# Fused attention and gated convolution on one core: attention products of a head pair moved into the next pair's slot, and all engines in written order

## The chip, the core and the metric

The program runs on one core of a Trainium2 chip. The core has a matrix engine (TensorE, PE in the profile; its weight loads are PEld), a vector engine (VectorE, DVE), an activation engine (ScalarE, ACT), a general engine (GpSimd, POOL) and SyncE (SP), which here only issues transfers. Each engine works through a list of instructions of its own and waits on semaphores for the others. The metric is the device time of one execution in microseconds (us); lower is better.

## What is computed

Eight batches, twelve heads, 448 positions, head width 64. An attention whose softmax has exp(-m) added to its denominator is followed by a projection into three parts, a circular convolution of the middle part along the sequence (written with FFTs), a product of the three parts, and an output projection:

```
scores = (1/sqrt(64)) * q @ k^T;  m = max(scores);  e = exp(scores - m)
attn   = e / (sum(e) + exp(-m) + 1e-09);   x = concat_heads(attn @ v)      # 8 x 448 x 768
x1, x2, x3 = split(x @ w_proj, 3)                                          # 768 -> 3*768
x2_conv = irfft(rfft(x2, axis=1) * rfft(filter_fft, axis=0), axis=1)
out = (x1 * x2_conv * x3) @ w_out
```

Multiplied through by exp(m), the denominator is 1 + sum(exp(scores)), so no maximum is taken. The FFTs are products with small sine and cosine tables.

## The kernel before

**Attention** goes by head pair `hp` (six to a batch). `transposes` (T in what follows) turns the pair's keys and queries by matmul into one PSUM tile and copies them with VectorE into a zero-padded key tile `kz` (two copies) and `qT`. `scores` is called four times: part 0 (S0) makes one matmul and one exp on ScalarE (`er`), parts 1 to 3 (S) two matmuls and one exp each (`e`); `er` and `e` are the numerators, transposed. `attn_out` (AV) is called for two halves of the queries: 14 matmuls into the tile `op`, of which there is one, then on VectorE `rec` (add 1, reciprocal) and the product `xb`. `back` (X, the way back) transposes `xb` and copies it into `xT`; GpSimd copies two columns of `xT`, and after every third pair VectorE folds `xT` into `xf` (`u`, `w`, four `xf` products: the folds).

**Dense work** of a batch is a list of units: 12 gate units (G: six matmuls of 448 columns; part 0 copied by ScalarE to `x1`, part 1 multiplied by VectorE into `g`), 8 projections (P: six matmuls of 384 columns, copied by ScalarE to `x2`), 4 spectrum units (Z: two matmuls, two ScalarE copies `xs`, four VectorE products into `yh`), 6 inverse units (V: four matmuls, ScalarE copy `cw`, and for each two of them three VectorE steps into `yT`) and 8 output units (W: six matmuls, ScalarE copy `osb`, a store for each two).

**PSUM**: two tiles for scores, one for `op`, three (tag `hy`) which T, X and all dense units share in turn.

**Order.** The main loop at the end walks through the attention units and after each takes dense units of the batch before from `queue`, in proportion to costs written by hand (RATIO 1.9). In a slot of a pair stand S0, T of the next pair, S, X of the pair before, S, S, AV, AV. `manual_schedule` keeps this order for TensorE and GpSimd; a scheduler orders VectorE, ScalarE and SyncE by its own estimate. Dense work of batch b starts in the first slot of batch b+1, once `filter_spectrum` (16 matmuls on a filter that is loaded by DMA, and its sums `uw` on VectorE) is done. After the last attention slot the dense work of batch 7 runs alone.

**Start.** `first_load` brings batch 0 as float32 through SyncE in per-pair tiles (three buffers to a kind); `first_casts` turns them into bf16 (keys VectorE, queries ScalarE, values GpSimd). `tables` makes the sine tables with VectorE and ScalarE. The later batches (`attn_load`), the weights and the filter come by casting DMAs from GpSimd's queue. Batch 0 has no dense work beside it.

Of the kernel before, what the change touches and what calls it, by code (L numbers as in the profile page):

```python
# [19 lines left out]
SP = 112  # L20
# [19 lines left out]
def kernel(  # L40
# [33 lines left out]
    make_identity(nc, ident_bf)  # L74
# [15 lines left out]
    for i in range(2):  # L90
        nc.vector.memset(kn[i][:, :, 0, :], 0.0)
        nc.vector.memset(vr[i], 0.0)
        nc.vector.memset(vn[i][:, :, :, DH : DH + 1], 1.0)
        for u in range(2):
            nc.vector.memset(vr[i][64 * u : 64 * u + 64, :, u, DH : DH + 1], 1.0)
    for i in range(3):
        nc.vector.memset(kz[i], 0.0)
# [34 lines left out]
    def first_load(sp, tp):  # L132


        A = batch_tiles(0)
        rows = {}
        for name, x in (("k", k), ("v", v)):
            y = rows[name] = x[0].rearrange("h s d -> (h s) d").rearrange("(g r) d -> r g d", r=896)
            R = A[f"s{name}r"] = tp.tile([128, NHP, DH], F32, name=f"s{name}r")
            nc.sync.dma_start(R, y[384:512])  # L140
        for hp in range(NHP):
            for name in ("k", "v"):
                t = A[f"s{name}", hp] = sp.tile([128, 2, 3, DH], F32, name=f"s{name}")
                for u in range(2):
                    nc.sync.dma_start(
                        t[:, u].rearrange("p j d -> p (j d)"),
                        rows[name][512 * u : 512 * u + 384, hp, :].rearrange(
                            "(p j) d -> p (j d)", j=3
                        ),
                    )  # L150
                if name == "k":
                    t = A["sq", hp] = sp.tile([SP, 2, NST, DH], F32, name="sq")
                    nc.sync.dma_start(
                        t[:].rearrange("p u j d -> p u (j d)"),
                        q[0, 2 * hp : 2 * hp + 2].rearrange("u (p j) d -> p u (j d)", j=NST),
                    )
        return A

    def first_rests(A):
        for u in range(2):  # L160
            c = slice(64 * u, 64 * u + 64)
            nc.vector.tensor_copy(A["kn"][c, :, 0, c], A["skr"][c])
            nc.gpsimd.tensor_copy(A["vr"][c, :, u, 0:DH], A["svr"][c])

    def first_casts(A, hp):
        nc.vector.tensor_copy(
            A["kn"][:, hp, 1:4, :].rearrange("p j (u d) -> p u j d", u=2), A["sk", hp]
        )
        nc.scalar.copy(
            A["qf"][:, :, 2 * hp : 2 * hp + 2, :].rearrange("p j u d -> p u j d"), A["sq", hp]  # L170
        )
        for u in range(2):
            nc.gpsimd.tensor_copy(
                A["vn"][:, hp, 4 * u : 4 * u + 3, 0:DH], A["sv", hp][:, u]
            )
# [99 lines left out]
    def filter_load():  # L275
        F = hyp.tile([FQ, 4, D], BF16, name="filt", tag="yh")
# [8 lines left out]
    def filter_spectrum(F):  # L285

        uw = hyp.tile([FQ, 2, 2, D], BF16, name="uw", tag="g")
# [26 lines left out]
    def transposes(A, hp):  # L314
# [18 lines left out]
        if A["b"] == 0:  # L333
# [48 lines left out]
    def back(A, hp):  # L382
# [9 lines left out]
        nc.gpsimd.tensor_copy(xT[:, hp, S : S + 2], xT[:, hp, 0:2])  # L392
        if hp % 3 == 2:
            ds = slice(hp - 2, hp + 1)
            u = fold.tile([128, 3, HALF + 2], BF16, name="u")
            w = fold.tile([128, 3, HALF + 2], BF16, name="w")
            lo, hi = xT[:, ds, 0 : HALF + 2], xT[:, ds, HALF : S + 2]
            nc.vector.tensor_tensor(u, lo, hi, op=ALU.add)
            nc.vector.tensor_tensor(w, lo, hi, op=ALU.subtract)
            for pg, (t, op) in enumerate(  # L400
                ((u, ALU.add), (u, ALU.subtract), (w, ALU.subtract), (w, ALU.add))
            ):
                nc.vector.tensor_tensor(
                    A["xf"][:, pg, ds, 0:FQ],
# [229 lines left out]
```

## Time and profile before

| | |
|---|---|
| median of three runs | 532.7 us (531.22 to 533.28) |
| profiled execution | 532.04 us, of which 530.3 us are the span of the profile |
| PE / PEld busy | 439.5 us (83%) / 299.5 us |
| DVE / ACT / POOL busy | 303.4 us (57%) / 292.7 us (55%) / 117.6 us (22%) |
| exp of a score pair `e` (L348), of `er` (L352) | 920 ns x144, 550 ns x48 |
| `rec` add (L373), reciprocal (L374), `xb` (L375) | 160, 176, 424 ns x96 each |
| folds `u` (L398), `w` (L399), `xf` (L403) | 509, 505 ns x16; 334 ns x64 |
| `xs` copy (L460), `x1` copy (L484), `g` product (L486) | 485, 537, 618 ns |
| first scores, batch 0: pair 0, pair 2, pair 3 | start at 21.28, 46.06, 53.20 us |
| matmuls of `filter_spectrum` | 76.02 to 79.53 us |
| memsets of one `kn`, `vr`, `vn` on VectorE | 0.38, 0.71, 0.09 and two in 0.19 us |

The mean durations are those of a group of like instructions. Neighbours on an engine overlap a little at their ends, so that starts lie closer together than the durations say. An idle time is put down to the engine or transfer whose semaphore came last. The granted clock of TensorE is a share of 2.4 GHz: 0.78 between 20 and 40 us, 0.71 between 40 and 60, 0.91 between 60 and 80, and 1.00 from there to 500 us.

### The profile page before, as it was taken

Reading aid. Unit: us, or ns where it says so; the run is one execution under the profiler, and the core shown is the slowest. Engines: PE = TensorE matmul, PEld = TensorE weight load, DVE = VectorE, ACT = ScalarE, POOL = GpSimd, SP = SyncE. Lnnn points to the kernel's source line nnn. Section 1 sums busy time; section 2 is a strip of 40 time slices with the busy share of each in tenths; the row PEclk is TensorE's granted clock in tenths of the full one; section 3 lists DMA queues with packets and bytes.
Section 4 is the critical chain, followed back from the end, with each engine's and each line's share of the span. In section 5 each row is a group of like instructions: output and inputs, shape, how many; then the busy total and the mean of one; then the engine's idle time right before and its main releaser. Section 6 shows DMA issues by size and latency. Waiting matters only on the chain.

```text
span 530.3 us, 9720 instructions
## 1 busy us (share of the span) xinstructions
PE 439.5 (83%) x3872; PEld 299.5 (56%) x3872; DVE 303.4 (57%) x881; ACT 292.7 (55%) x499; POOL 117.6 (22%) x184
## 2 busy tenths in 40 slices
PE   0254678989997899989997999989997999899995
PEld 0133456556664676556664667557664667466654
DVE  8624653685529744675538644674548654774170
ACT  2532465656565574665565565755665656745443
POOL 4447026000530018010620027000710000000000
PEclk9966899999999999999999999999999999999999
DMA  7999919300990039601990049401990030002003
GB/s 214 207 208 127 123 10 133 17 2 28 131 103 2 2 105 123 36 0 54 126 84 1 2 112 131 19 1 54 142 70 1 6 99 1 2 1 79 26 1 104
DMA packets 128685, 35.63 MB, mean 67 GB/s; under 512 B 117117, under 2 KB 125056, under 8 KB 128640
## 3 DMA queue, kind: packets, MB, share of 16 engines
q0 software_dynamic: 118080, 19.87, 50.1%
q1 hardware_dynamic: 10560, 15.14, 9.6%
q8 instruction: 30, 0.49, 0.4%
q14 instruction: 15, 0.12, 0.1%
HBM read 43.86 MB, written 11.01 MB: 103 GB/s over the span
## 4 chain that ended last, share of the span: by engine, by line
PE 52%; DVE 21%; ACT 13%; DMA 6%; issue 5%; SPq 1%; POOL 1%; ACTq 0%; DVEq 0%; POOLq 0%
PE ops L523 11%; PE pps L440 11%; PE pps L475 10%; ACT e L348 8%; PE op L365 6%; PE sc L346 5%; ACT cw L506 3%; DVE t L463 3%; DVE t L464 3%; DMA filt<-in_moe_filter_fft_dram 2%; PE op L360 2%; DVE xb L375 2%; PE xps L388 2%; DMA sv<-in_v_dram 2%; DVE g L486 2%
## 5 line engine op out<-in xcount | busy, mean ns | idle before, releaser
L348 ACT ACTIVATE e<-sc 128x896 bf16<-128x896 f32 x144 | 129.6, 920 | 20.5 <-PE sc L346 19.0
L475 PE MATMUL pps<-xT,wproj_bf 128*128 128x448 bf16 x576 | 124.0, 352 | 0.2 <-DVE g L486 0.2
L392 POOL COPY xT<-xT 128x2 bf16<-128x2 bf16 x48 | 11.1, 234 | 344.0 <-DVE xT L391 336.1
L346 PE MATMUL sc<-qT,kz 128*128 128x448 bf16 x288 | 78.6, 365 | 4.5 <-ACT e L348 4.5
L365 PE MATMUL op<-vn,e 128*128 128x65 bf16 x1152 | 66.6, 197 | 17.3 <-ACT e L348 17.3
L523 PE MATMUL ops<-wout_bf,yT 128*112 128x384 bf16 x384 | 73.3, 328 | 8.4 <-DVE yT L514 8.4
L475 PEld LDWEIGHTS <-wproj_bf 128*128 128x128 bf16 x576 | 53.8, 97 | 46.4 <-issue 0.8
L440 PE MATMUL pps<-wproj_bf,xf 128*113 128x384 bf16 x384 | 72.0, 327 | 0.0
L365 PEld LDWEIGHTS <-e 128*128 128x128 bf16 x1152 | 54.5, 99 | 26.6 <-ACT e L348 22.2
L360 PE MATMUL op<-vr,er 128*128 128x130 bf16 x192 | 43.1, 225 | 27.6 <-DVE xb L375 27.6
L373 DVE TENSOR_SCALAR rec<-op 128x4 f32<-128x4 f32 x96 | 15.4, 160 | 86.2 <-PE op L365 84.9
L523 PEld LDWEIGHTS <-yT 128*112 128x112 bf16 x384 | 47.1, 130 | 23.7 <-DVE yT L514 11.2
L440 PEld LDWEIGHTS <-xf 128*113 128x113 bf16 x384 | 48.4, 132 | 12.6
L352 ACT ACTIVATE er<-sc 128x448 bf16<-128x448 f32 x48 | 26.4, 550 | 48.0 <-PE sc L350 48.0
L530 ACT COPY osb<-ops 112x384 f32<-112x384 f32 x64 | 30.7, 479 | 40.2 <-PE ops L523 34.3
L506 ACT CAST cw<-cps 128x448 bf16<-128x448 f32 x48 | 24.6, 534 | 50.8 <-PE cps L499 34.8
L486 DVE TENSOR_TENSOR g<-x,pps 128x448 bf16<-128x448 bf16 x48 | 29.7, 618 | 39.5 <-PE pps L475 39.5
L447 ACT CAST x<-pps 113x384 bf16<-113x384 f32 x64 | 30.7, 480 | 34.7 <-PE pps L440 34.3
L360 PEld LDWEIGHTS <-er 128*128 128x128 bf16 x192 | 18.9, 99 | 44.5 <-DVE xb L375 40.8
L375 DVE TENSOR_TENSOR xb<-op,rec 128x256 bf16<-128x256 f32 x96 | 40.7, 424 | 3.2
L346 PEld LDWEIGHTS <-kz 128*128 128x128 bf16 x288 | 26.8, 101 | 18.4 <-issue 7.4
L391 DVE COPY xT<-xps 128x448 bf16<-128x448 bf16 x48 | 18.8, 393 | 31.6 <-PE xps L388 31.6
(94 smaller groups left out, 603.2 us busy)
## 6 DMA issues: line engine op xcount, KB each, us to landing
out_dram<-osb SPq DMA_DIRECT2D x32, 336.0 KB, 2.7
qf<-in_q_dram POOLq DMA_DIRECT2D x28, 168.0 KB, 5.3
vn<-in_v_dram POOLq DMA_DIRECT2D x7, 672.0 KB, 9.3
kn<-in_k_dram POOLq DMA_DIRECT2D x42, 96.0 KB, 4.8
wproj_bf<-in_moe_w_proj_dram POOLq DMA_DIRECT2D x3, 1152.0 KB, 15.3
sq<-in_q_dram SPq DMA_DIRECT2D x6, 224.0 KB, 3.9
sk<-in_k_dram SPq DMA_DIRECT2D x12, 96.0 KB, 3.4
sv<-in_v_dram SPq DMA_DIRECT2D x12, 96.0 KB, 3.6
```

Source lines behind the costliest of these rows:

```text
L346: nc.tensor.matmul(sc[:, u, 0:S], P["z"][:, (4 - t, 4 + t)[u], :], P["qT"])
L348: nc.scalar.activation(e, sc[:, :, 0:S], AF.Exp, scale=SCALE)
L360: nc.tensor.matmul(op[:, i, :, :], e[0][:, qs], A["vr"][:, hp, :, :], start=True, stop=False)
L365: nc.tensor.matmul(op[:, i, u, :], e[1 + t][:, u, qs], A["vn"][:, hp, 4 * u + t, :], start=False, stop=(u == 1 and t == 2),)
L375: nc.vector.tensor_tensor(A["xb"][:, 2 * hf : 2 * hf + 2, 2 * hp : 2 * hp + 2, :], op[:, :, :, 0:DH], rec[:].unsqueeze(3).to_broadcast([12 ...
L440: nc.tensor.matmul(pps[:FQ, :DCH], xf[:, pg, kt, 0:FQ], wproj_bf[:, kt, D + ch * DCH : D + (ch + 1) * DCH], start=(kt == 0), stop=(kt == N ...
L447: nc.scalar.copy(T["x2"][:, pg, ch * DCH : (ch + 1) * DCH], pps[:FQ, :DCH])
L475: nc.tensor.matmul(p[:, :S], wproj_bf[:, kt, 2 * part * D + dt * 128 : 2 * part * D + (dt + 1) * 128], xT[:, kt, 0:S], start=(kt == 0), st ...
L486: nc.vector.tensor_tensor(T["g"][:, dt, :], T["x1"], p[:, :S], op=ALU.mult)
L506: nc.scalar.copy(cw[:, dt % 2, :, :], cps[:, 0:S].rearrange("p (a n) -> p a n", a=2))
L523: nc.tensor.matmul(ops_[:SP, :DCH], yT[:, dt, st * SP : (st + 1) * SP], wout_bf[:, dt, ch * DCH : (ch + 1) * DCH], start=(dt == 0), stop=( ...
L530: nc.scalar.copy(osb[:, ch * DCH : (ch + 1) * DCH], ops_[:SP, :DCH])
```

## The change

**Attention.** A slot now holds S0, S and then the products of the pair *before*: AV (first half), T of the next pair, S, AV (second half), S, X of the pair before, and after every third pair the folds, which are units of cost 0 of their own. The two columns of `xT` are copied by VectorE in the first fold unit, for three pairs at a time, where GpSimd did it for each pair. One more slot at the end holds what is left of the last pair.

**Order.** VectorE and ScalarE are now in the manual schedule too, so that they work in the order in which the program emits the instructions.

**Dense units.** Spectrum units stand between projections and gates, inverse units between gates; the first store's two output tiles are taken together, four of six matmuls each first, the last two of each in a second unit (`write_out`). The other six output units are as before (`plain_out`).

**Start.** The cast of a pair's tiles is emitted at the head of the slot of the pair before; keys and queries are both cast by VectorE (queries of pair 0 by ScalarE). The tables stand ahead of all casts. `first_load` is now `staged_load`, with one DMA for both heads of a key or value tile where there were two. Memsets of `kn`, `vn`, `vr` go to GpSimd, those of the second buffer later. `filter_spectrum` is emitted after X of the last pair of batch 0, no longer in the first slot of batch 1 after S. The weights, filter and batch 1 are loaded from the slots of pairs 1, 2 and 4.

```diff
@@ main loop
+        tc.manual_schedule(engines={E.PE, E.Pool, E.DVE, E.Activation}),
-        state = {0: first_load(sp, tp)}
+        state = {0: staged_load(0, sp, tp)}
+        make_identity(nc, ident_bf)
+        constants(0)
+        for z in kz:
+            nc.vector.memset(z, 0.0)
         tables(tp)
...
+        cast_k(A, 0, nc.vector)
+        cast_shared(A, "k", nc.vector)
+        cast_q(A, 0, nc.scalar)
+        cast_v(A, 0, nc.gpsimd)
+        cast_shared(A, "v", nc.gpsimd)
+        transposes(A, 0)
+        for cost, (what, b, hp, part), emit in attention():
+            if what == "S" and part == 0:
+                if b == 0 and hp + 1 < NHP:
+                    cast_k(A, hp + 1, nc.vector)
+                    cast_q(A, hp + 1, nc.vector)
+                    cast_v(A, hp + 1, nc.gpsimd)
+                if b == 0 and hp == 1:
+                    wproj_load(1)
+                    constants(1)
+                if b == 0 and hp == 2:
+                    wproj_load(0)
+                    wproj_load(2)
+                if b == 0 and hp == 4:
+                    F = filter_load()
+                    state[1] = attn_load(1)
+                    wout_load()
...
+            emit()
+            if what == "X" and hp == NHP - 1:
+                if b == 0:
+                    filter_spectrum(F)
+                queue += dense(state[b])
@@ attention(), one slot
+            sc(0)
+            sc(1)
+            av(0)
+            if nxt:
+                units.append((0.42, ("T", *nxt, 0), lambda c=nxt: transposes(state[c[0]], c[1])))
+            sc(2)
+            av(1)
+            sc(3)
+            if old:
+                units.append((0.23, ("X", *old, 0), lambda c=old: back(state[c[0]], c[1])))
+            for part in range(3):
+                fd(part)
@@ dense(), order of the units (G gate, P proj2, Z spectrum, V inverse)
+        U = [G(0, 0), G(0, 1)]
+        U += [P(pg, ch) for pg in range(2) for ch in range(2)]
+        U += [P(2, 0), Z(0, 0), P(2, 1), P(3, 0), Z(0, 1), P(3, 1)]
+        U += [G(1, 0), Z(1, 0), G(1, 1), G(2, 0), Z(1, 1), G(2, 1), G(3, 0), G(3, 1)]
+        U += [V(0), G(4, 0), V(1), G(4, 1), V(2), G(5, 0), V(3), V(4), G(5, 1), V(5)]
+        U += [(1.29, lambda: write_out(0, 0)), (0.65, lambda: write_out(0, 1))]
-        U += gu(1)
-        for par in range(2):
-            for ch in range(2):
-                U.append((0.33, lambda par=par, ch=ch: spectrum(par, ch)))
-            U += gu(2 + par)
...
```

Three places show what this moves. The first is **VectorE after the second pair's products**: before, the filter's sums `uw` (L288, L289) stand between the second pair's way back (`xT`) and its own products (`rec`, `xb`).

```order
L391 COPY xT<-xps 128x448
L288 TENSOR_TENSOR uw<-filt 113x1536
L373 TENSOR_SCALAR rec<-op 128x4
L289 TENSOR_TENSOR uw<-filt 113x1536
L374 RECIPROCAL rec<-rec 128x4
L375 TENSOR_TENSOR xb<-op,rec 128x2x128
```

In the changed program the same sums (now L295, L296) stand behind the way back of batch 0's last pair, in the first slot of batch 1:

```order
L380 TENSOR_SCALAR rec<-op 128x4
L381 RECIPROCAL rec<-rec 128x4
L382 TENSOR_TENSOR xb<-op,rec 128x2x128
L398 COPY xT<-xps 128x448
L295 TENSOR_TENSOR uw<-filt 113x1536
L296 TENSOR_TENSOR uw<-filt 113x1536
L404 COPY xT<-xT 128x3x2
L408 TENSOR_TENSOR u<-xT 128x678
```

The sums moved behind four more pairs. The second place is **TensorE behind score matmuls** (batch 0, second pair, where no dense unit stands between; the numbers are those of the tiles). Before, the pair's own products follow its last score pair `sc_424`; of the numerators, `e_427` is the exp of just that pair:

```order
L346 LDWEIGHTS kz1_118
L346 MATMUL sc_424<-qT_333,kz1_118 128x448
L360 LDWEIGHTS er_392
L360 MATMUL op_429<-vr0_115,er_392 128x130
L365 LDWEIGHTS e_410
L365 MATMUL op_429<-vn0_113,e_410 128x65
L365 LDWEIGHTS e_422
L365 MATMUL op_429<-vn0_113,e_422 128x65
L365 LDWEIGHTS e_427
L365 MATMUL op_429<-vn0_113,e_427 128x65
```

In the changed program the second pair's first score pair `sc_343` is followed by products on the numerators of the first pair (`er_262` to `e_290`), which were all made in the slot before:

```order
L353 LDWEIGHTS kz1_114
L353 MATMUL sc_343<-qT_278,kz1_114 128x448
L367 LDWEIGHTS er_262
L367 MATMUL op_348<-vr0_111,er_262 128x130
L372 LDWEIGHTS e_267
L372 MATMUL op_348<-vn0_109,e_267 128x65
L372 LDWEIGHTS e_285
L372 MATMUL op_348<-vn0_109,e_285 128x65
L372 LDWEIGHTS e_290
L372 MATMUL op_348<-vn0_109,e_290 128x65
```

The products moved one slot back, and between their halves T and a score pair now stand. The third place is **VectorE in the slot with two spectrum units** (the third slot of every batch's dense work). Before, the scheduler had the products of an AV unit (`rec`, `xb`) and the copies of T (`kz`, `qT`) ahead of the spectrum's products (`t`, `yh`):

```order
L373 TENSOR_SCALAR rec<-op 128x4
L330 COPY kz_118<-tps 64x4x128
L374 RECIPROCAL rec<-rec 128x4
L331 COPY kz_118<-tps 64x512
L375 TENSOR_TENSOR xb<-op,rec 128x2x128
L338 COPY qT<-tps 128x448
L486 TENSOR_TENSOR g<-x_1210,pps_1229 128x448
L391 COPY xT<-xps 128x448
L463 TENSOR_TENSOR t_1249<-xs,hrs 112x768
L464 TENSOR_TENSOR t_1250<-xs,hrs 112x768
```

Now the first spectrum unit of that slot stands ahead of them:

```order
L496 TENSOR_TENSOR t_1155<-xs,hrs 112x768
L497 TENSOR_TENSOR t_1156<-xs,hrs 112x768
L498 TENSOR_TENSOR yh<-t_1155 112x384
L501 TENSOR_TENSOR yh<-t_1156 112x384
L380 TENSOR_SCALAR rec<-op 128x4
L381 RECIPROCAL rec<-rec 128x4
L382 TENSOR_TENSOR xb<-op,rec 128x2x128
L519 TENSOR_TENSOR g<-x_1137,pps_1180 128x448
L337 COPY kz_114<-tps 64x4x128
L338 COPY kz_114<-tps 64x512
L345 COPY qT<-tps 128x448
L496 TENSOR_TENSOR t_1222<-xs,hrs 112x768
```

The spectrum's four products moved ahead of the AV chain, the gate product and T's copies.

## Rows read from the trace of the kernel before

**Rows 1.** Matmuls by start (us), duration, engine, line: first dense gates of batch 0, batch 7
```profile
79.53 1.30 PE L475 MATMUL pps<-xT,wproj_bf 128*128 128x448 bf16 x6
...
489.43 2.44 PE L475 MATMUL pps<-xT,wproj_bf 128*128 128x448 bf16 x12
```
**Rows 2.** Busy time of a stretch of one batch: start:end, length, busy time by engine, clock
```profile
200.73:259.60 58.87, 53.09 (x483) 36.34 (x482) 35.09 (x103) 34.94 (x60) 14.36 (x22) 1.00 0.65 60
```
**Rows 3.** Waits of TensorE in that stretch: who waits for whom, us, times, longest
```profile
PE op L360 <- DVE xb L375: 2.0, 2, 1.0
...
PE op L365 <- ACT e L348: 1.8, 4, 0.9
...
PE ops L523 <- DVE yT L514: 1.0, 1, 1.0
...
PE xsp L459 <- DVE qT L338: 0.7, 1, 0.7
```
**Rows 4.** Time line near 43 us: the filter's sums, and TensorE's next matmul
```profile
42.69 0.96 DVE L288 TENSOR_TENSOR uw<-filt 113x1536 bf16<-113x1536 bf16 x1 [8.27 <-DMA filt<-in_moe_filter_fft_dram]
...
45.19 0.29 PE L360 MATMUL op<-vr,er 128*128 128x130 bf16 x1 [8.77 <-DVE xb L375]
```
**Rows 5.** Time line of VectorE in a pair of batch 0 (products, copies of T, way back)
```profile
46.29 0.16 DVE L373 TENSOR_SCALAR rec<-op 128x4 f32<-128x4 f32 x1 [1.16 <-PE op L365]
...
47.46 0.42 DVE L330 COPY kz<-tps 64x512 bf16<-64x512 bf16 x1 [0.34 <-PE tps L322]
...
48.34 1.16 DVE L334 COPY qT<-tps 128x448 bf16<-128x448 bf16 x1
49.30 0.41 DVE L391 COPY xT<-xps 128x448 bf16<-128x448 bf16 x1
```
**Rows 6.** Casts of batch 0 by group: line, engine, shapes, count, busy us, mean ns
```profile
L169 ACT CAST qf<-sq 112x512 bf16<-112x512 f32 x6 | 3.7, 618 | 12.1 <-DMA sq<-in_q_dram 12.0
L166 DVE CAST kn<-sk 128x384 bf16<-128x384 f32 x6 | 2.5, 424 | 0.4 <-DMA sk<-in_k_dram 0.4
```
**Rows 7.** Time line of the tables: first step, end of the first range reduction, sine
```profile
5.93 0.26 DVE L184 CAST col<-ci 128x224 f32<-128x224 int32 x1
...
11.94 1.09 DVE L216 SCALAR_TENSOR_TENSOR pf<-rd,pf 128x904 f32<-128x904 f32 x1
...
15.14 0.96 ACT L220 ACTIVATE sn<-pf 128x904 f32<-128x904 f32 x1
```
**Rows 8.** Time line of GpSimd: a cast of values alone, and three beside the tables
```profile
6.78 0.34 POOL L173 CAST vn<-sv 128x192 bf16<-128x192 f32 x1 [1.17 <-DMA sv<-in_v_dram]
...
10.29 4.33 POOL L173 CAST vn<-sv 128x192 bf16<-128x192 f32 x3 [0.39 <-DMA sv<-in_v_dram]
```
**Rows 9.** Chain that ended last: start, us; a staged load beside the weights' loads
```profile
16.40 10.04 DMA sv<-in_v_dram
```
**Rows 10.** Time line of TensorE, steady: starts of AV, G, S0, P, T, S
```profile
200.06 0.23 PE L360 MATMUL op<-vr,er 128*128 128x130 bf16 x1 [0.93 <-DVE xb L375]
...
200.57 1.30 PE L475 MATMUL pps<-xT,wproj_bf 128*128 128x448 bf16 x6
201.71 0.35 PE L350 MATMUL sc<-qT,kz 128*128 128x448 bf16 x1
201.89 1.14 PE L440 MATMUL pps<-wproj_bf,xf 128*113 128x384 bf16 x6
202.87 0.39 PE L320 MATMUL tps<-ident_bf,kn 128*128 128x128 bf16 x4
...
203.29 0.54 PE L346 MATMUL sc<-qT,kz 128*128 128x448 bf16 x2
```
**Rows 11.** Time line of VectorE: the same step of two spectrum units back to back
```profile
219.15 0.56 DVE L463 TENSOR_TENSOR t<-xs,hrs 113x768 bf16<-113x768 bf16 x1
...
220.63 0.55 DVE L463 TENSOR_TENSOR t<-xs,hrs 113x768 bf16<-113x768 bf16 x1
```
**Rows 12.** Time line of TensorE at the end: the last output units
```profile
518.76 7.36 PE L523 MATMUL ops<-wout_bf,yT 128*112 128x384 bf16 x44 [1.28 <-DVE yT L514]
```

More of the change, by code (lines that the diff above doesn't have):

```diff
@@ L514, in inverse, with write_out, plain_out @@
                 nc.vector.tensor_tensor(yT[:, ds, :], g[:, ds, :], cv, op=ALU.mult)
-        def write_out(st, ch):
+        def write_out(st, part):
+            yT = T["yT"]
+            if part == 0:
+                T["osb"] = otp.tile([SP, D], F32, name="osb")
+                T["ops"] = [phy.tile([128, 512], F32, name="ops", tag="hy") for _ in range(2)]
+            osb = T["osb"]
+            for ch in range(2):
+                for dt in (range(4), range(4, 6))[part]:
+                    nc.tensor.matmul(
+                        T["ops"][ch][:SP, :DCH],
+                        yT[:, dt, st * SP : (st + 1) * SP],
+                        wout_bf[:, dt, ch * DCH : (ch + 1) * DCH],
+                        start=(dt == 0),
+                        stop=(dt == NDT - 1),
+                    )
+            if part == 0:
+                return
+            for ch in range(2):
+                nc.scalar.copy(
+                    osb[:, ch * DCH : (ch + 1) * DCH], T["ops"][ch][:SP, :DCH]
+                )
+            nc.sync.dma_start(out[b, st * SP : (st + 1) * SP, :], osb)
+        def plain_out(st, ch):
             yT = T["yT"]
@@ L576 @@
-        F = filter_load()
-        state[1] = attn_load(1)
-        wout_load()
-        transposes(state[0], 0)
-        queue, owed = [], 0.0
-        for b in range(n_batches):
-            for i, (cost, emit) in enumerate(attention(b)):
-                emit()
-                if b and i == 5:
-                    if b == 1:
-                        filter_spectrum(F)
-                    queue += dense(state[b - 1])
-                if i == 8 and b and b + 1 < n_batches:
+        state = {0: staged_load(0, sp, tp)}
@@ L601 @@
-        back(last, NHP - 1)
-        for c, f in queue + dense(last):
+            emit()
[3 more added lines that the diff above has]
+                queue += dense(state[b])
+            if not queue:
+                owed = 0.0
+                continue
+            owed += cost * RATIO
+            while queue and owed >= queue[0][0] / 2:
+                c, f = queue.pop(0)
+                f()
+                owed -= c
@@ L603 @@
+        for c, f in queue:
             f()
```

200 lines of the change are left out of this document (93 added, 107 removed).

## Prediction

> **What bounds the kernel now.** I read the time line for the two marks that cut the run into three parts: the first dense gate of batch 0 starts at 79.53 us, that of batch 7 at 489.43 [rows 1]. So there is a start of 79.5, a middle of 409.9 and a tail of 530.3 - 489.4 = 40.9 us. The middle repeats every 58.87 us: seven times that is 412.1, and the last round lacks score and T units worth 2.2. Then I read busy time in one round. TensorE is busy 53.09 of 58.87 us at full clock, VectorE and ScalarE 35 each [rows 2]: TensorE sets the middle, and the most a new order can win there is 5.8 us a round. The waits say where these lie [rows 3]: 2.0 on `xb` (the second AV half needs the one `op` tile back from VectorE), 1.8 on the exp just issued, 1.0 on `yT` ahead of the output units, 0.7 on T's copies, for which a spectrum unit waits to get a PSUM tile. The start is another matter: TensorE is mostly idle there, and one wait alone is 8.8 us long: VectorE stood at the filter's sums, whose DMA landed at 42.7, and the products of the second pair stood behind them [rows 4].
>
> **The change, part by part. The start.** (a) Tables. They now stand ahead of every cast on VectorE. To the end of the first range reduction took 5.93 to 13.03, with two key casts (0.42 each) in between [rows 6, 7]: 6.3 us without them. Sine and its hand-over cost 1.1 [rows 7], the two scalings 0.9, and a second round of reduction, sine and scaling 4.3 (as much as the same steps took in the first): 12.6 in all. They need GpSimd's column numbers, which now wait for a set of memsets (1.4 us on VectorE): from 5.93 [rows 7] I move their start to 3.6 and their end to 16.2. Key casts, T and its copies (1.84 [rows 5]) add 4.4: first score at 20.6, where it was 21.3. A wash; bounds 19 to 24.
>
> (b) Pairs of batch 0. No dense work runs, and the chain now goes round through VectorE, whose order is fixed: two chains `rec` to `xb` of 0.83 (160 + 176 + 424 ns and two hand-overs), T's copies 1.84, `xT` 0.41 [rows 5], key cast 0.42 and query cast 0.56 (not seen on VectorE; the key cast scaled from 384 to 512 columns, between 0.35 and ScalarE's 0.62 [rows 6]): 4.9 us. It waits twice for TensorE: from `xb` through X to `xT` 0.6, and from the casts to the end of the next AV half 0 to 0.7. That is 5.9 a pair (5.5 to 6.3), after 7.1 before (first scores at 46.06 and 53.20). The products come a slot later, so X of pair 0 ends at 20.6 + 10.0, then four slots of 5.9, one of them 1.3 longer by the folds; the last two are lighter (no casts, T's plain copy: 5.1). X of pair 5 is then at 30.6 + 2 x 5.9 + 7.2 + 2 x 5.1 = 59.8.
>
> (c) Filter. The sums now stand behind that X: 0.8 for `xT`, 0.96 + 0.87 for the sums, 0.1 to hand over. The 8.8 us wait is gone, since the DMA had landed by 42.7 and is issued some 10 us sooner; but the 16 matmuls (76.0 to 79.5 before, 3.5) follow only now. First gate: 59.8 + 2.7 + 3.5 = 66.0, bounds 61 to 74. **Gain 13.5.**
>
> (d) Transfers. GpSimd's queue no longer waits for late staged values, so the weights go out some 5 us sooner and run beside the keys of pairs 3 to 5, which SyncE can issue only when VectorE's casts free the buffers (from 16.6 on). A staged load beside the weights took 10.0 us [rows 9], so the keys of pair 3 land at 27; their cast is due at 31, and later pairs have more room. Hidden; without that cover the cast, first in VectorE's order, holds up everything by what is missing. Batch 1 is issued behind them and due at 55. One DMA for two saves SyncE 0.5 each, hidden.
>
> (e) GpSimd beside VectorE. Three casts of values took 4.33 us beside the tables, one alone 0.34 [rows 8]: the two engines hold each other up there. The Trainium skill's page "SBUF — State Buffer", section "Who interferes with whom", says that they share one pair of ports, which one instruction holds exclusively to its end, whoever starts first. By the row the loss falls on GpSimd, which has 15 us to spare; by the rule VectorE, which now has the tables on the path, could lose as much, up to 12 waits of 0.4 us: first gate at 71. This lies inside the bounds.
>
> **The middle.** (f) AV on numerators of the slot before: the waits of 1.8 on the exp go. Between the halves stand T, a score pair and one to two dense units, 0.42 + 0.36 + 1.0 at least [rows 10], where the chain through `xb` takes 1.0: the 2.0 go. X needs the second half's `xb`; a score pair and a dense unit (1.3) stand ahead of it, so nothing new. Score tiles come back in time: between the fourth and the next slot's second score unit lie about 1.6 us for an exp of 0.92.
>
> (g) Output units: four of six matmuls of the first two tiles (1.3 us) now hide the `yT` chain, so the 1.0 goes.
>
> (h) Spectrum units. This is the price. In the slot with two of them VectorE's order is now: four products, AV chain, `g`, T's copies, four products. The first products wait for `xs`, which ScalarE makes behind `er` and `e`: 2.2 us after the score pair ends (0.55 + 0.92 less overlap, two copies of 0.4, hand-overs). From there 1.48 [rows 11] + 0.83 + 0.55 + 1.25 run to the end of T's copies: 6.3. TensorE in that time has Z 0.3, AV 0.5, G 1.14, T 0.42, G 1.14, S 0.36 [rows 10], 3.9 in all, and then wants T's PSUM tile: it waits 2.4, where before the same tile cost 0.7. Bounds: nothing, if ScalarE is early, to 4.5, if the other slot with spectrum units waits as much. I take 2.4, as every link has a row.
>
> Round: 58.87 - 1.8 - 2.0 - 1.0 + 1.7 = 55.8; waits that I can't place (new ones on `hy` tiles) 0.1, so **55.9, bounds 54.0 to 58.5, gain 3.0 a round, 20.8 in seven.**
>
> (i) `xT`'s two columns go from GpSimd to VectorE, once for three pairs; 16 small copies of some 0.15 us, off the path.
>
> **The tail.** TensorE waits 1.28 for `yT` [rows 12] and 0.4 at each of four spectrum pieces. Half an output unit more stands in front of the first, and one unit between the others: I take back 1.4 of 2.9. The new last slot hides its chains behind the three output units that are left over, as before. Tail 39.5, bounds 38.5 to 41.
>
> **Sum.** 66.0 + (7 x 55.9 - 2.2) + 39.5 = 494.6 us of span. Around the span lie 532.04 - 530.3 = 1.7, and the median stands 0.7 above the profiled execution: **497.0**.
>
> **Rivals.** A: the forecast, 497 by the likely values. B: the middle keeps its period, since the fixed order of VectorE and ScalarE gives new waits for those that it removes; 66.0 + 409.9 + 39.5 + 2.4 = 518. For it: the scheduler had put AV's chain and T's copies ahead of spectrum products, and now a waiting product blocks them. Against: only two of six slots have that pattern. C, on the other side: the same convoy in all four spectrum units and behind both folds. It decides when waits in a round exceed 5.8 + (13.5 + 1.4) / 7 = 7.9 us, more than three times the 2.4 that I place; with 2.4 for each of the four units the round is 53.1 + 9.6 = 62.7: 66.0 + 436.7 + 39.5 + 2.4 = 545. The page "PSUM — Partial Sum Buffer", section "Engine vs sequencer instructions", says that the queues of ScalarE and VectorE are strictly first in, first out; that is the mechanism of this rival, and rows 4 show it at work, 8.8 us for one instruction. D: the weights' flood reaches the staged keys: a load of 20 us, twice [rows 9], puts the key cast of pair 3 six us late and the next as well; first gate at 76: 507. E: no wait in the middle at all but some tenths, because ScalarE and VectorE run ahead of my hand count; period 53.6: 481.
>
> **How the numbers follow.** A 0.60 (488 to 508), B 0.10, C 0.06, D 0.10, E 0.14. The range leaves out C, the lower part of E and the upper edge of B: 482 to 517. A measurement of this kernel can tell about 0.5% (2.7 us) from no change. Slower by more than that is C, 0.06; within it the narrow way from B to C, 0.03; faster 0.91.
>
> **What would show it.** The first gate (its line is L508 after) near 66 and the first score near 20.6; the filter's sums without a long DMA wait ahead of them. A round of 55.9 with TensorE still busy 53.1; no waits of AV on exps or `xb`; one of about 2.4 us at a spectrum matmul on T's copies. The tail at 39.5. It is wrong if VectorE's casts wait for DMAs between 20 and 50 us (D), if TensorE's waits in a round on VectorE add up to more than 5 us (B, C), or if the first score comes after 24.

## Result and profile after the change

The changed kernel takes **474.5 us** (median of four, 472.71 to 475.23) beside 533.0 us of the kernel before in the same session: a ratio of 0.890 (95% interval 0.887 to 0.894). The prediction was 497.0 us, in a range of 482 to 517: the direction was right, the gain was 58.5 us where 35.7 had been forecast. Cut at the marks that the prediction used, the profiled executions read:

| us | before | forecast | after |
|---|---|---|---|
| first dense gate of batch 0 | 79.5 | 66.0 | 65.8 |
| from there to the first gate of batch 7 | 409.9 | 389.1 | 367.0 |
| of that, one round | 58.87 | 55.9 | 52.61 |
| tail | 40.9 | 39.5 | 40.1 |
| span | 530.3 | 494.6 | 472.9 |

Start and tail came out near the forecast in their sums. The whole miss of 21.7 us of span is in the middle: the middle came out 22.1 shorter than forecast, the two ends together 0.4 longer.

The time line of TensorE (start, duration, engine, line, operation) has the two marks, as [rows 1] has them for before:

```profile
65.76 1.30 PE L508 MATMUL pps<-xT,wproj_bf 128*128 128x448 bf16 x6
...
432.77 2.06 PE L508 MATMUL pps<-xT,wproj_bf 128*128 128x448 bf16 x10
```

Busy time in one round of after, columns as in [rows 2] (start:end, length, PE, PEld, DVE, ACT, POOL, clock, DMA):

```profile
119.00:171.61 52.61, 51.62 (x484) 36.67 (x482) 35.34 (x105) 34.73 (x61) 13.04 (x16) 1.00 0.73 67
```

TensorE's waits in that round, all that the view lists:

```profile
PE xsp L492 <- DVE g L519: 0.5, 1, 0.5
PE xsp L492 <- ACT x L517: 0.2, 1, 0.2
```

Against [rows 3] the waits on `xb`, on `e`, on `yT` and on T's `qT` are all gone. What is left are two waits of a spectrum unit, 0.7 us together. TensorE idles 0.99 us a round, and its **busy** time is 1.47 us less than in [rows 2] for the same work. The tail keeps one wait on `yT`, 0.53 us, ahead of the last part of the first output unit, where [rows 12] had 1.28:

```profile
461.77 0.86 PE L558 MATMUL ops<-wout_bf,yT 128*112 128x384 bf16 x4 [0.53 <-DVE yT L547]
```

In the start, the filter's sums follow the way back of the last pair at once, and TensorE waits 1.35 us for them, not 8.8 as in [rows 4]:

```profile
59.98 0.39 DVE L398 COPY xT<-xps 128x448 bf16<-128x448 bf16 x1 [0.38 <-PE xps L395]
60.29 0.95 DVE L295 TENSOR_TENSOR uw<-filt 113x1536 bf16<-113x1536 bf16 x1
...
61.30 0.32 PE L303 MATMUL hps<-uw,ft 113*113 113x384 bf16 x1 [1.35 <-DVE uw L295]
```

### The profile page after: what moved, and what is told of

The parts are those of the page before. It is cut to its first block, busy times and chain, and to the rows that moved or that the text cites. A ratio compares the mean times of both kernels' runs of the same rounds, so it can differ in the third digit from the quotient of the medians.

```text
span 472.9 us, 9624 instructions
## 1 busy us (share of the span) xinstructions
PE 426.3 (90%) x3872; PEld 298.9 (63%) x3872; DVE 307.3 (65%) x892; ACT 288.2 (61%) x493; POOL 109.4 (23%) x146
## 4 chain that ended last, share of the span: by engine, by line
PE 67%; DVE 14%; ACT 7%; DMA 7%; POOL 3%; issue 1%; SPq 1%; ACTq 0%; DVEq 0%; POOLq 0%
PE pps L508 18%; PE pps L473 10%; PE ops L580 10%; PE sc L353 9%; PE op L372 5%; DMA wproj_bf<-in_moe_w_proj_dram 4%; PE ops L558 3%; ACT xs L493 3%; PE cps L532 2%; PE xsp L492 2%; DVE t L496 2%; PE xps L395 2%; DVE g L519 2%; PE op L367 2%; DVE t L497 2%; ACT e L355 2%
## 5 line engine op out<-in xcount | busy, mean ns | idle before, releaser
L355 ACT ACTIVATE e<-sc 128x896 bf16<-128x896 f32 x144 | 132.6, 922 | 46.7 <-PE sc L353 46.7
L372 PE MATMUL op<-vn,e 128*128 128x65 bf16 x1152 | 58.1, 195 | 0.0
L372 PEld LDWEIGHTS <-e 128*128 128x128 bf16 x1152 | 51.4, 98 | 6.8 <-issue 0.7
L580 PE MATMUL ops<-wout_bf,yT 128*112 128x384 bf16 x288 | 53.8, 327 | 0.5 <-ACT osb L568 0.5
L115 POOL DMA_DIRECT2D qf<-in_q_dram x28 | 26.2, 943 | 120.8 <-PE tps L329 84.1
L517 ACT CAST x<-pps 128x448 bf16<-128x448 f32 x48 | 25.5, 532 | 28.9 <-PE pps L508 26.5
L580 PEld LDWEIGHTS <-yT 128*112 128x112 bf16 x288 | 35.8, 130 | 10.1 <-issue 0.6
L327 PE MATMUL tps<-ident_bf,kn 128*128 128x128 bf16 x192 | 19.5, 224 | 22.1 <-DVE kn L164 18.9
L496 DVE TENSOR_TENSOR t<-xs,hrs 113x768 bf16<-113x768 bf16 (+1 forms) x32 | 17.8, 556 | 32.6 <-ACT xs L493 32.6
L587 ACT COPY osb<-ops 112x384 f32<-112x384 f32 x48 | 23.0, 480 | 23.9 <-PE ops L580 21.3
```

The source lines that it names most:

```text
L115: nc.gpsimd.dma_start(A["qf"][:, st, :, :], q[b, :, st * SP : (st + 1) * SP, :].rearrange("h p d -> p h d"),)
L355: nc.scalar.activation(e, sc[:, :, 0:S], AF.Exp, scale=SCALE)
L372: nc.tensor.matmul(op[:, i, u, :], e[1 + t][:, u, qs], A["vn"][:, hp, 4 * u + t, :], start=False, stop=(u == 1 and t == 2),)
L496: nc.vector.tensor_tensor(t1[:K], xs[:K], hrs[:K, par, :, cs], op=ALU.mult)
L580: nc.tensor.matmul(ops_[:SP, :DCH], yT[:, dt, st * SP : (st + 1) * SP], wout_bf[:, dt, ch * DCH : (ch + 1) * DCH], start=(dt == 0), stop=( ...
```

## Experiments

The change has four parts that can be taken apart: the **deferral** (AV, X and folds in the next pair's slot), the **written order** of VectorE and ScalarE, the new **dense order** with the split first output unit, and the new **start**. In what follows "before" is some 532 us in every session.

### Which part made the gain in the middle

**a_av_own: everything but the deferral.** AV goes back behind the pair's own scores, X and the folds to their old places (units abbreviated).

```diff
             sc(0)
+            if nxt: T
             sc(1)
-            av(0); T; sc(2); av(1); sc(3); X(old)
+            X(old); sc(2); sc(3)
+            av(0); av(1)          # of the pair itself
```

> The changed kernel with one part undone: the AV products, their way back and the folds stand again in the slots in which they stood before (S0, T of the next pair, S, X of the pair before, S, S, AV, AV); all engines stay in written order, dense units and start stay as changed. Theory 1 (the middle was won by AV on numerators of the slot before, which takes away waits of TensorE on exps and on xb, and each such wait also costs about 0.16 us of drained matmul pipeline that the profile counts as busy): the round goes from 52.6 to about 57 us, with six to eight waits of AV on exps and xb and TensorE busy near 52.6, and the time to about 505 us. Rival (the middle was won by the written order of VectorE and ScalarE): the round stays below 54 and the time below 485 us.

Measured: 531.8 us, ratio 0.998 (0.996 to 1.001). The round was 58.83: the middle has gained nothing, although dense order, split and written order were all in. The start has gained little too: the first gate came at 77.6 us (79.5 before, 65.8 after).

```profile
136.72:195.55 58.83, 53.34 (x484) 36.30 (x482) 35.85 (x106) 34.79 (x61) 13.04 (x15) 1.00 0.63 60
```

```profile
PE op L367 <- DVE xb L382: 2.5, 3, 1.6
PE op L372 <- ACT e L355: 2.3, 5, 0.6
```

The waits of [rows 3] on `yT`, and of the spectrum unit on T's copies, are gone here too (X waits 0.3 for T's copies instead), but those on `xb` and `e` have grown from 3.8 to 4.8 us. As long as AV follows the exps of its own pair, the time saved elsewhere in this slot is waited away there. The deferral was worth more than I had expected even after the result.

**b_defer: the deferral alone, in the kernel before.** Scheduler, start, dense order, output units and folds stay (edit abbreviated).

```diff
+            sc(0); sc(1); av(old, 0); T; sc(2); av(old, 1); sc(3); X(old)
-                if b and i == 5:
+                if b and i == 7:
-        back(last, NHP - 1)
+        attn_out(last, NHP - 1, 0)
+        attn_out(last, NHP - 1, 1)
+        back(last, NHP - 1)
```

> The kernel before with one change: AV of a pair stands in the slot of the pair after it, between the score units as in the changed kernel, X behind the last score unit; the filter's matmuls and the dense work of a batch begin behind X of its last pair. VectorE and ScalarE stay with the scheduler, the start, the dense order, the output units and the folds are as before. Theory (deferral alone carries the middle): a round of 53 to 54.3 us with waits on e and xb gone, first gate near 81, the end 41: 81 + 7 x 53.6 - 2 + 41 + 2 = 497 us (492 to 503). Rival (deferral pays only together with the new dense order or the written order of VectorE and ScalarE): round 56 to 58, 515 to 528 us.

Measured: 496.2 us, ratio 0.932 (0.930 to 0.935). The first gate comes at 70.7 us, 8.8 earlier than in the kernel before, which I had not expected (81). The ring of a pair, the steps that wait for one another from one pair to the next, is shorter in batch 0 too: from one `xT` to the next (51.44 to 56.34 us) it takes 4.9 us, where it took 7.1 before (49.30 to 56.43). The round is 54.90, the tail 40.9.

```profile
125.62:180.52 54.90, 52.03 (x483) 36.43 (x482) 34.88 (x103) 34.58 (x61) 14.64 (x21) 1.00 0.70 64
```

```profile
PE ops L530 <- DVE yT L521: 1.6, 1, 1.6
PE xps L388 <- DVE xb L375: 0.5, 1, 0.5
PE xsp L466 <- ACT xs L467: 0.4, 1, 0.4
PE xsp L466 <- DVE qT L338: 0.3, 1, 0.3
```

So the deferral alone brings 36 of the 58 us: 26 of the 43 that the middle gained, and 8.8 at the start. What is left in its round are the waits on `yT` and around the spectrum units, which the dense order was made for.

**a_dense and a_plain: the dense order and the split, behind the deferral.** a_plain is the changed kernel with the first output unit whole; a_dense has the old order of all dense units besides (added lines only; they replace those of the change).

```diff
# a_plain
-        U += [(1.29, lambda: write_out(0, 0)), (0.65, lambda: write_out(0, 1))]
-        for st in range(1, NST):
+        for st in range(NST):
# a_dense, besides
+        U += [P(pg, ch) for pg in range(4) for ch in range(2)]
+        U += [G(1, 0), G(1, 1)]
+        for par in range(2):
+            U += [Z(par, 0), Z(par, 1), G(2 + par, 0), G(2 + par, 1)]
+        U += [V(0), V(1), G(4, 0), G(4, 1), V(2), V(3), G(5, 0), G(5, 1), V(4), V(5)]
```

> The changed kernel with the first two output tiles taken whole, one after the other, as the other six are (no split into four and two of six matmuls). This undoes step (g) alone. By step (g) TensorE should wait for yT again ahead of the first output tile, about 1.0 us a round and again in the tail: 474.5 + 8 x 1.0 = 482.5 us. By the rival that the attention units which now stand between the last inverse unit and the first output unit hide the chain anyway, nothing changes: 474.5, within 1 us.

> The changed kernel with the dense units in the order of the kernel before (all projections, then gates, pairs of spectrum units, gates, pairs of inverse units) and whole output tiles; the products of attention stay in the next pair's slot. Theory: the deferral makes the gain and the new dense order only trims waits; spectrum and inverse units side by side wait for each other's copies and yT's wait is back, some 1.5 us a round with the modelled matmul ends: round near 54, 474.5 + 7 x 1.5 + 2 in the tail = 487 us. Rival: the new dense order carries half of the 6.3 us that a round gained, then round 55.8 and 499 us. Rival: it carries nothing, 474.5 to 476 us.

Measured: a_plain 479.8 us, ratio 0.901 (0.898 to 0.904); a_dense 496.2 us, ratio 0.932 (0.929 to 0.934).

```profile
116.74:170.20 53.46, 51.82 (x483) 36.57 (x482) 35.47 (x105) 34.81 (x61) 13.04 (x16) 1.00 0.72 66
```

```profile
121.27:176.96 55.69, 52.37 (x483) 36.35 (x482) 35.57 (x105) 34.73 (x61) 13.03 (x16) 1.00 0.69 63
```

The split is worth 0.85 us a round (one wait of 0.6 on `yT` is back), the order of the units another 2.2. That is more than I had expected of a_dense (round near 54): in written order the pairs of spectrum units also wait 1.0 for each other's copies `xs`, X 0.6 for `xb`, T and the inverse units 0.4. Dense order and split, worth nothing ahead of the deferral (a_av_own), are worth 3.1 us a round behind it. Both times VectorE and ScalarE work in written order; no run has the new dense order without the deferral under the scheduler.

**a_sched and b_fifo: the written order.** a_sched gives VectorE and ScalarE of the changed kernel back to the scheduler; b_fifo puts them in written order in the kernel before.

```diff
# a_sched
-        tc.manual_schedule(engines={E.PE, E.Pool, E.DVE, E.Activation}),
+        tc.manual_schedule(engines={E.PE, E.Pool}),
# b_fifo: the reverse, in the kernel before
```

> The changed kernel with VectorE and ScalarE given back to the scheduler; all else as changed. Theory 1: the round stays near 53 to 54 us, as AV still stands on numerators of the slot before; only the start may lose some us if the scheduler pulls the filter's sums or the casts forward; 475 to 488 us. Rival (written order won the middle): the round goes back to 57 or more and the time above 505 us.

> The kernel before with one part of the change alone: VectorE and ScalarE in written order too; attention slots, dense units and start code as before. Theory 1: the filter's sums go behind the fifth pair and the 8.8 us wait at 36 to 45 us goes, the middle keeps a round of 58 to 60 us with its waits on exps and xb: 520 to 528 us. Rival: the round falls below 56 us and the time below 505 us.

Measured: a_sched 476.7 us, ratio 0.896 (0.894 to 0.897), with the first gate at 71.3 and a round of 52.22. b_fifo 544.3 us, ratio 1.022 (1.018 to 1.025), with the first gate at 91.3 and a round of 58.85. In the middle the written order is worth nothing or costs 0.4 us a round, as a_sched's row shows beside that of after:

```profile
123.64:175.86 52.22, 51.47 (x483) 36.73 (x482) 35.51 (x106) 34.63 (x61) 13.03 (x16) 1.00 0.73 67
```

My expectation for b_fifo missed on the start. There the casts of all six pairs now stand ahead of the first exp, where the old program emits them; ScalarE's last query cast starts at 38.56 us, and the first score comes at 38.74, not 21.28. The chain that ended last shows what the casts wait for:

```profile
18.29 6.97 DMA sq<-in_q_dram
25.32 13.22 DMA sq<-in_q_dram
```

The changed program emits each cast a slot ahead, and there the written order wins 5.5 us of the start (65.8 against 71.3, where the chain of a_sched has 8.6 us of the filter's DMA).

### Why the spectrum units did not wait for T's tile

Step (h) let the three `hy` tiles go strictly in turn. In the slot concerned, the time lines of TensorE and VectorE of the changed kernel are:

```profile
141.87 0.32 PE L492 MATMUL xsp<-x,ft 113*112 113x384 bf16 x1 [0.24 <-ACT x L517]
142.65 0.32 PE L492 MATMUL xsp<-x,ft 113*112 113x384 bf16 x1 [0.46 <-DVE g L519]
142.81 0.22 PE L367 MATMUL op<-vr,er 128*128 128x130 bf16 x1
```

```profile
141.98 0.61 DVE L519 TENSOR_TENSOR g<-x,pps 128x448 bf16<-128x448 bf16 x1
...
143.38 0.39 DVE L345 COPY qT<-tps 128x448 bf16<-128x448 bf16 x1
```

VectorE's order is the one forecast, and T's copies end at 143.77. But the second spectrum matmul starts at 142.65, when the gate product `g` has ended: it has been given the gate's tile, not T's. **a_turn** is the changed kernel with the three tiles under names of their own, taken strictly in turn:

```diff
-    phy = ... tc.tile_pool(name="phy", bufs=3, ...)
+    phy = ... tc.tile_pool(name="phy", bufs=1, ...)
+    def hy(name):
+        turn[0] += 1
+        return phy.tile([128, 512], F32, name=name, tag=f"hy{turn[0] % 3}")
```

> The changed kernel with the three shared PSUM tiles handed out strictly in turn (three pools of one tile, used one after the other in the order of emission), where the allocator now gives the next taker whichever tile it reckons free first. If the prediction's step on spectrum units failed because it took the tiles to go strictly in turn, the second spectrum unit of the slot with two of them now waits some 2 to 2.5 us for T's copies, the round goes from 52.6 to 54.3 or more and the time to about 487 us. If it failed because ScalarE's copies come sooner than it counted, the round stays within 0.3 us of 52.6 and the time near 475 us.

Measured: 486.2 us, ratio 0.913 (0.910 to 0.917). The wait that I had forecast is there in every batch. In all (who waits for whom, us, times, longest), and in one slot:

```profile
PE xsp L498 <- DVE g L525: 7.4, 8, 1.0
PE xsp L498 <- DVE qT L351: 6.6, 8, 0.9
```

```profile
197.44 0.32 PE L498 MATMUL xsp<-x,ft 113*112 113x384 bf16 x1 [1.02 <-DVE g L525]
198.61 0.37 PE L498 MATMUL xsp<-x,ft 113*112 113x384 bf16 x1 [0.85 <-DVE qT L351]
```

So the mechanism of (h) exists, at 1.9 us (1.02 + 0.85) in place of 2.4, and the choice of tiles in the changed kernel avoids most of it. Even the links of (h) come out: from the end of the score pair (192.35, where the next matmul starts) to the end of T's copies (198.56) it is 6.2 us, forecast 6.3. The time agrees better than the reasoning deserves: the waits make a round 53.67 us, 1.06 longer, 7.4 in seven; the other 5 come from three rounds like the second row here, in which the clock is lower:

```profile
120.11:173.78 53.67, 51.53 (x483) 36.57 (x482) 35.53 (x105) 34.83 (x61) 13.03 (x16) 1.00 0.71 66
173.78:229.11 55.33, 53.19 (x484) 37.10 (x482) 35.62 (x105) 34.84 (x61) 13.04 (x16) 0.97 0.69 64
```

### What sets a pair of batch 0

**c_start** keeps the written order for VectorE and ScalarE only until the filter's matmuls, to join the start of after with the middle of a_sched. **c_load** is the changed kernel with batch 1 loaded ahead of the weights. **c_q** is c_start with the query casts on ScalarE, **c_best** is c_q with the loads of c_load.

```diff
# c_start
-        tc.manual_schedule(engines={E.PE, E.Pool, E.DVE, E.Activation}),
+        tc.manual_schedule(engines={E.PE, E.Pool}),
+        first = tc.manual_schedule(engines={E.DVE, E.Activation}); first.__enter__()
                     filter_spectrum(F)
+                    first.__exit__(None, None, None)
# c_load: slot of pair 1   constants(1); attn_load(1)
#         slot of pair 2   filter_load(); wproj_load(0)
#         slot of pair 4   wproj_load(2); wproj_load(1); wout_load()
# c_q
-                    cast_q(A, hp + 1, nc.vector)
+                    cast_q(A, hp + 1, nc.scalar)
```

> The changed kernel with VectorE and ScalarE in written order only as far as the filter's matmuls in the first slot of batch 1; from there on the scheduler orders them, as in a_sched. If the start owes its length to the written order and the middle nothing to it, the first gate stays near 65.8 us, the round is 52.2 (a_sched) where it was 52.6, and the time is 474.5 - 3.3 = 471.2 us. If the scheduler spreads work of the middle into the start, or the middle of a_sched owed its speed to another state of the tiles, it is 474 to 477 us.

> The changed kernel with the transfers of batch 1 issued in the slot of pair 1, the filter and the first third of the projection weights in that of pair 2, and the other two thirds with the output weights in that of pair 4. In the changed kernel GpSimd stood 6.5 and 6.9 us at batch 1's queries until weights had landed, and T of batch 1 waited 1.2 us for keys that landed at 51.3 us. If that is on the path, the keys land by 45 us, the first gate comes at 64 to 64.6 us (65.8), and the time is 473 us. If the slots of batch 0 go by VectorE's order anyway: 474.5. If the many small packets of batch 1's keys push back the staged tiles of pairs 3 to 5, casts on VectorE wait for transfers and it is 476 to 480 us. If the weights now land after the first gates want them, the first gate or the first projection waits for a DMA.

> c_start (written order for VectorE and ScalarE only until the filter's matmuls, the scheduler after that) with the query casts of pairs 1 to 5 on ScalarE. A pair of batch 0 took 4.89 us, of which VectorE had nothing to do for 0.4 only, its query cast is 0.42 us, and ScalarE idles 1.1 us there. If VectorE's chain sets these pairs, each of five loses 0.3 to 0.4 us: first gate near 63.8 us and 471.7 - 1.7 = 470.0 us. If TensorE's unclocked matmuls or the exp set them, or if the cast on ScalarE holds up the exp behind it, nothing changes: 471.7 us.

> c_q with the transfers in the order of c_load. If both parts of the start are on the path one behind the other: 471.7 - 1.7 - 1.2 = 468.8 us, first gate near 62.6. If the faster pairs only run into the staged tiles' transfers, VectorE's casts wait for a DMA in pairs 3 to 5, and it is as c_q or slower, 470 to 473 us.

Measured: c_start 471.7 us, ratio 0.885 (0.883 to 0.888), first gate 65.4: as expected. c_load 471.6 us, ratio 0.885 (0.882 to 0.889), first gate 64.0; by its interval it can't be told from the changed kernel (0.887 to 0.894). c_q 470.9 us, ratio 0.885 (0.882 to 0.887), first gate 64.5, which can't be told from c_start. c_best **468.1 us**, ratio 0.879 (0.876 to 0.882), first gate 64.1: faster than before, after and c_start.

What the two start edits are worth by themselves is not shown. In the changed kernel T of batch 1 waited for keys:

```profile
51.38 0.61 PE L327 MATMUL tps<-ident_bf,kn 128*128 128x128 bf16 x4 [1.17 <-DMA kn<-in_k_dram]
```

But a_plain, a_dense, a_turn and c_start, which issue the loads in the same order as the changed kernel, have no such wait (nor has c_load; c_q waits 0.8); their first gates come at 63.3, 65.6, 65.6 and 65.4 us, and a_plain's is earlier than c_load's. From the first `xT` of batch 0 to the last it is 25.9 us in c_load (32.24 to 58.14) and in c_start (33.76 to 59.68). So c_load's earlier first gate can't be put down to the keys. c_best was forecast at a first gate of 62.6; its time came out (468.8 forecast), its first gate did not, and where its 2.8 us over c_q lie the profiles, with first gates 0.5 apart, do not show.

That c_q gained nothing shows where my picture of a pair was wrong. VectorE's time line of a pair in c_q:

```profile
31.94 0.39 DVE L398 COPY xT<-xps 128x448 bf16<-128x448 bf16 x1 [0.38 <-PE xps L395]
32.25 0.42 DVE L169 CAST kn<-sk 128x384 bf16<-128x384 f32 x1
33.00 0.16 DVE L380 TENSOR_SCALAR rec<-op 128x4 f32<-128x4 f32 x1 [0.33 <-PE op L372]
...
36.83 0.39 DVE L398 COPY xT<-xps 128x448 bf16<-128x448 bf16 x1 [0.38 <-PE xps L395]
```

And in after:

```profile
31.98 0.39 DVE L398 COPY xT<-xps 128x448 bf16<-128x448 bf16 x1 [0.38 <-PE xps L395]
...
36.87 0.39 DVE L398 COPY xT<-xps 128x448 bf16<-128x448 bf16 x1 [0.38 <-PE xps L395]
```

From one `xT` to the next it is 4.89 us in both, in c_q with the query cast gone and 0.33 us of waiting in its place. The casts lie beside TensorE's part of the ring (X's second half, S0, S, AV's first half, 1.3 us); the ring is that and VectorE's row from `rec` to the second `xb`, 3.5 us. **c_ring** tests this: c_best with the query casts back on VectorE, and one of T's key copies on ScalarE (in batch 0; the later batches keep the old copy).

```diff
+        if "staged" in A:
+            nc.scalar.copy(z[64:128, 4:8, :], tk[64:128])
```

> c_best with the query casts back on VectorE, and of T's copies in batch 0 the second half of the keys (0.43 us) on ScalarE. c_q showed that a pair stays at 4.89 us without the query cast. My reading: the pair is a ring of VectorE's two AV chains and T's copies between them, 3.5 us in a row, and X's second half, S0, S and AV's first half on TensorE, 1.2 us; casts lie beside TensorE's part. Then a copy taken out of the ring shortens each pair by its 0.43 us, to 4.45 to 4.55, though the casts are back; four to five pairs give 1.7 to 2.1 us, 466.2 us. If ScalarE's exps (3.3 us a pair and now the copy) or TensorE's unclocked matmuls set the pair, it stays at 4.89 or grows, 468 to 469 us. The difference is near what the times can tell, so the pair's length in the trace decides.

Measured: 473.1 us, ratio 0.886 (0.883 to 0.888), slower than c_best. The two copies do not run side by side: ScalarE's begins when VectorE's has ended, and `qT` waits for ScalarE's.

```profile
33.43 0.39 DVE L401 COPY xT<-xps 128x448 bf16<-128x448 bf16 x1 [0.38 <-PE xps L398]
...
36.29 1.15 DVE L344 COPY qT<-tps 128x448 bf16<-128x448 bf16 x1 [0.65 <-ACT kz L339]
...
38.52 0.39 DVE L401 COPY xT<-xps 128x448 bf16<-128x448 bf16 x1 [0.38 <-PE xps L398]
```

The pair did not get shorter, but the run speaks for the ring: 0.43 us taken out of it and 0.65 put in make 0.22, and this pair grew by 0.20, to 5.09. That is a small part of the 5.0 us by which c_ring is slower than c_best; 3.6 of them lie in the start (first gate at 67.7), 1.1 of these in the filter's matmuls, which took 4.8 us from the first start to the last, 3.7 in c_best. Whether a copy that truly ran beside would shorten the pair stays open.

## Why the prediction was right and wrong

Two steps failed, both about the middle. They make the 3.3 us by which a round was missed: 1.5 by the first and 1.8 by the second. Either of them put right alone would still have given more than was measured, 486.7 us (497.0 less seven times 1.47) or 484.4.

**The first step that failed: "the most a new order can win there is 5.8 us a round."** The new order won 6.3 (58.87 less 52.61). I took TensorE's busy 53.09 of [rows 2] as a floor. It is none. Here are eight kernels with the same matmuls in a round, by the windows shown above, all at full clock, with the number of waits of TensorE that the view lists:

| kernel | round | idle | waits | busy |
|---|---|---|---|---|
| before | 58.87 | 5.78 | 9 | 53.09 |
| a_av_own | 58.83 | 5.49 | 10 | 53.34 |
| a_dense | 55.69 | 3.32 | 7 | 52.37 |
| b_defer | 54.90 | 2.87 | 4 | 52.03 |
| a_plain | 53.46 | 1.64 | 3 | 51.82 |
| a_turn | 53.67 | 2.14 | 2 | 51.53 |
| after | 52.61 | 0.99 | 2 | 51.62 |
| a_sched | 52.22 | 0.75 | 2 | 51.47 |

The ninth wait of before is one that [rows 3] leave out:

```profile
PE xps L388 <- DVE g L486: 0.2, 1, 0.2
```

Busy time goes with the number of waits and not with their length: a_turn idles twice as long as after, in as many waits, and is no busier. From two waits to ten it grows by some 1.8 us, 0.2 a wait. The rows at 142.65 and 142.81 above show what this is likely to be: the single spectrum matmul is listed with 0.32 us, and the next instruction starts 0.16 later. In a row of matmuls such an end lies beside the next matmul; ahead of a wait it stands alone and is counted as busy. Seven waits fewer make 1.1 us of the 1.47 by which after is less busy than before; this is argued from these rows and not isolated, and where the rest lies stays open.

**The second: step (h), the spectrum units' wait, was mis-sized.** It was forecast at 2.4 us, and 0.70 was measured, as much as [rows 3] had. The order on VectorE was read rightly; what failed is that TensorE "then wants T's PSUM tile". That the tiles go in turn was taken for granted, and a_turn shows that it decides: with tiles in turn the wait is 1.9. With the 0.1 for waits not placed, this is the other 1.8 us. My bounds for (h), "nothing" to 4.5, did hold it.

**Steps (f) and (g) were right.** AV's waits on `e` and `xb` went with the deferral alone (b_defer), and the split took the wait on `yT` (a_plain). What I had missed is that these parts are not a sum: ahead of the deferral the others are worth nothing (a_av_own). Behind it dense order and split are worth 3.1 us a round, and a_dense, with written order, new start and new folds, has a round 0.8 longer than b_defer, which has none of these.

**The start was right in its sum and wrong in its parts.** (a) The first score came at 21.97 us, not 20.6. The tables ended 0.6 after the forecast (16.76 for 16.2); the key casts of the shared rows took 1.64 us for two, beside casts and DMA issues of GpSimd. (b) A pair took 4.89 us, not 5.9. I had added up VectorE's whole work, 4.9, and then two waits for TensorE, 1.0. VectorE's row took 4.5 with its hand-overs, and one wait of 0.38 is left: the casts and `xT` fill the second, as c_q shows for the query cast. (The text of (b) speaks of four slots of 5.9; its sum has two of them, one of 7.2 and two of 5.1, the five that are needed.) (c) The four us won in four such pairs were given back: 1.4 by the first score; 2.0, where 1.3 had been allowed for the folds, by T, which waited for a key cast behind them on VectorE; 1.2 by T of batch 1, which waited for keys; 0.8 by the filter's matmuls, 4.3 us in place of 3.5, with the granted clock of 60 to 66 us at 0.72. So 65.8 against 66.0 is partly luck. (d) No cast on VectorE waited for a DMA, as said; but batch 1's keys landed only at 51.3, as GpSimd stood 6.5 and 6.9 us at the queries until weights had landed. That cost 1.2 us here; a_plain, a_dense, a_turn and c_start, with the same order of loads, did not pay it.

**Rivals.** B (518: a middle that keeps its period) is what a_av_own's middle does without the deferral; with the deferral it is refuted. C (545, the convoy: an instruction that waits holds up all behind it) did not come in the middle: a_sched without the written order has a round of 52.22 against 52.61, so the written order costs 0.4 us. It did come in b_fifo's start, 12 us. The Trainium skill's page "PSUM — Partial Sum Buffer", section "Engine vs sequencer instructions", has the queues of ScalarE and VectorE strictly first in, first out; b_fifo's start agrees with it. D is refuted by (d). E (481, a round of 53.6) was the nearest, and even it kept the false floor: 53.1 busy and 0.5 idle.

**Tail.** 40.1 against 39.5: the wait on `yT` fell from 1.28 to 0.53, half of what I took back.

## What to carry to other kernels

When the busiest engine is in order and waits for results that it has just asked for, move the consumer one iteration back before polishing anything else: here, until that was done, what was saved elsewhere was waited away at that place. Do not read a busy time as a floor where the waits are many. An engine order written by hand is worth what its emission order is worth: here it won 5.5 us in a program that emits each cast a slot ahead, and cost 12 in one that does not.

## What the runs showed of the hardware

**VectorE loses beside GpSimd too.** The sum of step (e) let GpSimd alone pay. The same range reduction step (L222, 896 elements) took 0.65 us in the changed kernel and 1.80 in a_plain, where the memsets of the second buffers had slid beside it (in the changed kernel they start at 14.11). After, then a_plain with its memsets:

```profile
13.05 0.65 DVE L222 TENSOR_SCALAR rd<-rd 128x896 f32<-128x896 f32 x1
```

```profile
13.79 1.80 DVE L222 TENSOR_SCALAR rd<-rd 128x896 f32<-128x896 f32 x1
```

```profile
13.25 1.18 POOL L91 MEMSET kn<- 128x768 bf16 x1
14.38 0.74 POOL L92 MEMSET vr<- 128x780 bf16 x1
```

a_plain's first score came at 23.30 us and the changed kernel's at 21.97, though the start of the two is the same program. The Trainium skill's page "SBUF — State Buffer", section "Who interferes with whom", has the two share a pair of ports that either can hold to the end of its instruction; by that rule VectorE pays as well, and these rows agree with it, though no run isolates it. By it the start could also differ from kernel to kernel by which one comes first; the 1.3 us between the two first scores fit that and are not traced further.

**The granted clock fell behind a wait in some rounds and not in others.** In a_turn the same two waits (1.02 and 0.85 us) stand in every round. In the round from 173.78 us five gate matmuls right behind them then take 2.06 us, where six took 1.30 in the round before, and the granted clock of the round is 0.97, not 1.00: a stretch at the lower of the two levels (1.2 GHz).

```profile
145.63 1.30 PE L514 MATMUL pps<-xT,wproj_bf 128*128 128x448 bf16 x6
...
199.35 2.06 PE L514 MATMUL pps<-xT,wproj_bf 128*128 128x448 bf16 x5
```

What decides it no run here tells.
